# Interleaving four neighbouring tokens per partition in the attention stage of a fused attention, mixture-of-experts and feed-forward kernel

## Chip, cores and metric

The kernel runs on one core of one Trainium2 chip. The metric is the device time of one execution in microseconds (us). Three executions of the kernel before took 1749.69, 1757.17 and 1756.43 us, so the median is 1756.43.

## What is computed

```python
def _attn_ref(q, k, v):                       # (8, 8, 576, 64): batch, heads, tokens, head width
    k_p = k.reshape(B, H, 72, 8, D).mean(axis=3)
    v_p = v.reshape(B, H, 72, 8, D).mean(axis=3)
    scores = scale * np.matmul(q, k_p.transpose(0, 1, 3, 2))
    attn = softmax(scores)
    return np.matmul(attn, v_p)

x = attn_out.transpose(0, 2, 1, 3).reshape(B * S, H * D)      # 4608 tokens x 512
logits = x @ w_gate + np.log1p(np.exp(x @ w_noise)) * noise   # 8 experts, the best two are taken
out = sum over both: weight * (np.maximum(x @ w1[e], 0) @ w2[e])
h = out @ w_in;  g = h - np.tanh(h);  result = g @ w_out
```

Every token's row goes through attention, routing, its two experts and the last block by itself. The order in which tokens are put into tiles is therefore free, as long as the row of each token is read and written at its own place.

## The kernel before

The 4608 tokens are cut into 36 tiles of 128 tokens, one token per partition. A batch has 576 tokens, so a batch is 4.5 tiles long and two batches are nine tiles; tile 4 of each nine holds the end of one batch and the beginning of the next.

The program has three stages. `attention` (from line 1128) walks over the tiles and leaves each tile's 128 x 512 result in a DRAM buffer `x_d`, at row 128 t + partition. Beside it the router picks two experts per token and builds lists of row numbers. `moe` (from line 187) gathers rows of `x_d` by these lists, does the two layers of each expert and stores to `y_d`. `Moe2` (from line 659) gathers the two rows of each token, combines them and does the last block; line 1070 stores 128 result rows at a time to `out`.

The order of the work in `attention` is written out by hand in one loop over t (line 1713). One step t holds, among others: a load of q for tile t+4 (`load_q`, line 1184), the exponentials of tile t on ScalarE (`st_exps`, line 1362), the transposes of the attention weights of tile t-2 (`st_attT`, line 1387), the transposes of q of tile t+2 (`st_q`, line 1340), the scores of tile t+1 (`st_scores`, line 1348), jobs on k and v of a coming batch (line 1606 on), and the products with v of tile t-3 (`st_av`, line 1399). `st_g` (line 1421) scales the result of tile t-4 and stores it to `x_d`.

`load_q` issues one DMA on the queue of SyncE (SP) for each tile (two for a tile with two batches): 128 partitions x 8 heads x 64 elements, that is 1024 runs of 256 bytes. There are four buffers `qt`. The first four tiles are loaded ahead of the loop (lines 1207, 1208, 1237, 1240) between the loads of k and v of batches 0 and 1 (`load_kv`, line 1148). The noise of the router, 4608 x 8 numbers, is loaded at step 2 by one DMA (line 1662) in runs of 32 bytes.

In `st_q` the 512 columns of a q tile are transposed by four TensorE transposes of 128 x 128 (two heads each) into one PSUM tile `pt`, which ScalarE copies to `qT`:

```python
for m in range(HP):
    nc.tensor.transpose(p[:, m], qt[:, 2 * m:2 * m + 2].rearrange("s h d -> s (h d)"), identf)
QT[t] = wk.tile([128, HP, 128], F32, name="qT")
nc.scalar.activation(QT[t], p, AF.Copy)
```

A neighbour of it in form is `kbd` (line 1325), which multiplies a 64-column slice of the pooled k by a masked identity `parity`, so that the two products of a pair fill the lower and the upper 64 partitions of one PSUM tile (line 1331). The scores of a tile with two batches have the same form: 64-column slices of `qT`, lower and upper half in turn (line 1354).

SP's queue runs in program order and also carries the loads of k, v, weights and noise and the stores of `x_d`; each of its DMAs waits until the one eight before it has landed (the DMAHW entries in the order below).

Of the kernel before, what the change touches and what calls it, by code (L numbers as in the profile page):

```python
# [10 lines left out]
F32 = mybir.dt.float32  # L11
# [25 lines left out]
@with_exitstack  # L37
def kernel(ctx, tc, q, k, v, w_gate, w_noise, noise, w1, w2, w_in, w_out, out):
    nc = tc.nc
    B, H, S, D = q.shape  # L40
    N, E = noise.shape
    DM = H * D
    FF = w1.shape[2]
    F2 = w_in.shape[1]
    SP = S // 8
    NT = N // 128
    HP = H // 2
    ctx.enter_context(tc.manual_schedule())

    dram = ctx.enter_context(tc.tile_pool(name="dram", bufs=1, space=DRAM))  # L50
    x_d = dram.tile([N, DM], F32, name="x_d")
    y_d = dram.tile([(E + 1) * CAP + 128, DM], F32, name="y_d")
    ws_d = dram.tile([128, 2, 4, F2], F16, name="ws_d")
    const = ctx.enter_context(tc.tile_pool(name="const", bufs=1))

    identf = const.tile([128, 128], F32, name="identf")
    make_identity(nc, identf)
    onec = const.tile([128, 1], F32, name="onec")
    nc.vector.memset(onec, 1.0)
    ones1 = onec[0:1, 0:1].to_broadcast([1, 128])  # L60
    iota8 = const.tile([128, E], F32, name="iota8")
    nc.gpsimd.iota(iota8, pattern=[[1, E]], base=0, channel_multiplier=0, allow_small_or_imprecise_dtypes=True)
    tokid = const.tile([128, NT], I32, name="tokid")
    nc.gpsimd.iota(tokid, pattern=[[128, NT]], base=0, channel_multiplier=1)
    ridx = const.tile([128, NT, 2], I32, name="ridx")
    coef = const.tile([128, NT, 2], F32, name="coef")
    exps = const.tile([128, NT, 2, 1], F32, name="exps")
    poss = const.tile([128, NT, 2, 1], I32, name="poss")
    counts = const.tile([128, E], F32, name="counts")
    cnti = const.tile([1, 2 * E + 2], I32, name="cnti")  # L70
    idx = const.tile([128, E, NT], I32, name="idx")
    cin = const.tile([128, 4], F32, name="cin")
    wn2 = const.tile([1, 4], F32, name="wn2")
    outc = const.tile([128, DM], F32, name="outc")

    iscm = const.tile([128, 1], F32, name="iscm")
    hold = ctx.enter_context(tc.tile_pool(name="hold", bufs=1, side="right"))
    ew = ExitStack()
    early = ExitStack()
    pairs = [ew.enter_context(tc.tile_pool(name="ew0", bufs=1, side="right"))]  # L80
    ep = early.enter_context(tc.tile_pool(name="early", bufs=1, side="right"))
    x0T = ep.tile([128, 2, DM // 128, 512], F16, name="x0T")
    gate_ps = []
    W = {}
    V = dict(locals())
    with ExitStack() as st:
        attention(nc, tc, st, V)
    big = ctx.enter_context(tc.tile_pool(name="big", bufs=1))
    V["wi"] = big.tile([128, 2, 4, F2], F16, name="wi")
    V["wo"] = big.tile([128, 2, F2 // 128, DM], F16, name="wo")  # L90
    V["ps"] = ctx.enter_context(tc.tile_pool(name="m_ps", bufs=1, space=PSUM))
    z = Moe2(nc, tc, V)
    with ExitStack() as st:
        moe(nc, tc, st, V, z)
    ew.close()
    z.run(ctx)


def pow2(nc, m, x):
# [559 lines left out]
class Moe2:  # L659
# [165 lines left out]
    def main(self, near):  # L825
# [225 lines left out]
        def L2(j, f, blocks=range(4)):  # L1051
            g = G[j, f] if blocks[-1] < 3 else G.pop((j, f))
            for i in blocks:
                if f == 0:
                    PO[j, i] = ps.tile([128, DM], F32, name="py", bufs=4)
                p = PO[j, i]
                s = slice(128 * i, 128 * i + 128)
                nc.tensor.matmul(p, g[:, 0, s], wo[:, 0, f], start=(f == 0), stop=False)  # L1058
                nc.tensor.matmul(p, g[:, 0, s], wo[:, 1, f], start=False, stop=False)  # L1059
                nc.tensor.matmul(p, g[:, 1, s], wo[:, 0, f], start=False, stop=(f == KF - 1))  # L1060
            if f == KF - 1:
                for i in blocks:
                    o = wk.tile([128, DM], F32, name="o", bufs=5)
                    if i % 2:
                        nc.scalar.activation(o, PO.pop((j, i)), AF.Copy, scale=INV[j][:, i:i + 1])
                        tt(o, o, outc, op=OP.mult)
                    else:
                        stt(o, PO.pop((j, i)), INV[j][:, i:i + 1], outc, op0=OP.mult, op1=OP.mult)
                    r = 128 * (4 * j + i)
                    nc.sync.dma_start(self.out[r:r + 128, :], o)  # L1070

        if near:
            INV[0], ROW[0, 0] = self.first
# [8 lines left out]
        for u in range(len(units) + LAG):  # L1082
# [12 lines left out]
            if u < len(units):  # L1095
                j, f = units[u]
# [31 lines left out]
def attention(nc, tc, st, V):  # L1128
# [19 lines left out]
    def load_kv(b, nm, cs=((0, 3), (3, 5)), engs=(nc.sync,)):  # L1148
        a = KV[b, nm] = KVT[nm][b % 2]
        rows = dict(k=k, v=v)[nm][b].rearrange("h (s r) d -> (h s) r d", r=8)  # L1150
        for i, (c0, c1) in enumerate(cs):
            w = cuts[c1] - cuts[c1 - 1]
            engs[i % len(engs)].dma_start(a[:w, c0:c1], rows[cuts[c0]:cuts[c1]].rearrange("(c p) r d -> p c r d", p=w))
# [16 lines left out]
        a = KV[b, nm]  # L1170
        e.tensor_add(a[:, c, 0:n], a[:, c, 0:n], a[:, c, n:2 * n])

    QL = {}

    def runs(t):
        r, done = [], 0
# [4 lines left out]
            done += n  # L1181
        return r

    def load_q(t):
        qt = ld.tile([128, H, D], F32, name="qt", bufs=4)
        for o, n, b, s in runs(t):
            nc.sync.dma_start(qt[o:o + n], q[b, :, s:s + n, :].rearrange("h s d -> s h d"))
        QL[t] = qt

# [14 lines left out]
        for i in range(2):  # L1204
            nc.gpsimd.memset(KVT[nm][i][96:128, 3:5], 0.0)
    load_kv(0, "k", each, (nc.sync, nc.scalar))
    load_q(0)
    load_q(1)
    rowi = one.tile([128, 128], F32, name="rowi")
    nc.gpsimd.iota(rowi, pattern=[[1, 128]], base=0, channel_multiplier=-1, allow_small_or_imprecise_dtypes=True)  # L1210
    KB = [one.tile([128, 2 * HP * SP], F32, name=f"kb{i}") for i in range(2)]
# [22 lines left out]
    nc.gpsimd.iota(slot, pattern=[[1, 128]], base=0, channel_multiplier=0, allow_small_or_imprecise_dtypes=True)  # L1234
    lane = ep.tile([128, 1], F32, name="lane")
    nc.gpsimd.iota(lane, pattern=[[0, 1]], base=0, channel_multiplier=1, allow_small_or_imprecise_dtypes=True)
    load_q(2)
    load_kv(1, "k")
    load_kv(0, "v", each)
    load_q(3)  # L1240
    for w, o in ((w_gate, 0), (w_noise, E)):
        nc.sync.dma_start(wg[:, 0:H, o:o + E], w.rearrange("(h p) e -> p h e", p=64))
    load_kv(1, "v")
    nz = ep.tile([128, NT, E], F32, name="nz")
    for c in each:
# [94 lines left out]
    def st_q(t):  # L1340
        p = ps.tile([128, HP, 128], F32, name="pt", bufs=3)
        qt = QL.pop(t)
        for m in range(HP):
            nc.tensor.transpose(p[:, m], qt[:, 2 * m:2 * m + 2].rearrange("s h d -> s (h d)"), identf)
        QT[t] = wk.tile([128, HP, 128], F32, name="qT")
        nc.scalar.activation(QT[t], p, AF.Copy)

# [248 lines left out]
    def at(t, f, *a):  # L1596
        assert t >= 0
        at_step.setdefault(t, []).append((f, a))
# [38 lines left out]
    for b in range(1, B):  # L1637
# [21 lines left out]
        at_pe(T0, job["vt"])  # L1659
        at_pe(T0 + 1, job["vs"])  # L1660
        fixed(T0 + 1, 1800)
    at(2, lambda: nc.sync.dma_start(nz, noise.rearrange("(t p) e -> p t e", p=128)))

    def early_x():

# [46 lines left out]
    ex = []  # L1712
    for t in range(NT + 4):
        now[0] = t
        if t + 4 < NT:
            load_q(t + 4)
        if t < NT:
            st_exps(t)
        if t < 4:
# [89 lines left out]
```

## Time and profile before

| | |
|---|---|
| runs, us | 1749.69, 1757.17, 1756.43 (median 1756.43) |
| profiled execution | 1757.43 us, span 1755.6 us from the first to the last instruction |
| granted TensorE clock | 0.996 of full speed over the span |
| TensorE (PE) busy | 1723.1 us, 98% of the span |
| VectorE (DVE), ScalarE (ACT), GpSimd (POOL) busy | 1266.2, 922.9, 274.7 us |
| q loads | 40 DMAs on SP, 32 of 256 KB and 8 of 128 KB |
| last product of attention (line 1413) | starts at 208.89 us |
| first matmul of the experts (line 356) | starts at 211.72 us |

The profiled execution is 1.83 us longer than its span. An engine's busy time counts matmuls with modelled ends, so a PE that is busy need not be at its peak; how long a group of matmuls holds the PE is read from the start of its first to the start of the next group. Idle time of an engine is shown in square brackets with what ended it.

### The profile page before, as it was taken

What the parts mean: (1) busy time and instruction counts of PE and PEld (TensorE: products, weight loads), DVE (VectorE), ACT (ScalarE), POOL (GpSimd) and SP (SyncE); (2) the same over time, 40 slices, a digit from 0 to 9 for tenths busy, and PEclk for the clock granted to TensorE, in tenths of its full rate; (3) what the DMA queues carried; (4) which work ended last, traced back from release to release, by engine and by line L of the source; (5) the groups of instructions that cost most, each with busy time, mean ns of one, the idle gap of its engine ahead of it and who ended that gap; (6) DMA issues with size and microseconds to landing.
All of it is one profiled execution on the core that took longest, in us unless ns stands there. A gap on an engine that the chain in (4) does not pass through costs nothing.

```text
span 1755.6 us, 28446 instructions
## 1 busy us (share of the span) xinstructions
PE 1723.1 (98%) x10574; PEld 1040.4 (59%) x10576; DVE 1266.2 (72%) x2547; ACT 922.9 (53%) x2229; POOL 274.7 (16%) x267
## 2 busy tenths in 40 slices
PE   7999999999999999999999999999999999999997
PEld 5989855454454545445454544666666666666664
DVE  5789788766666676666564558688787978888775
ACT  5788634435243443434343446656575756657553
POOL 2443113131030301101010211102010101200000
PEclk9999999999999999999999999999999999999999
DMA  9998335645746464535643445223131304232100
GB/s 222 271 192 214 103 106 165 165 132 150 184 124 181 137 175 132 126 120 131 170 131 88 124 125 127 68 53 85 43 87 35 97 19 97 66 50 64 22 25 26
DMA packets 271413, 203.35 MB, mean 116 GB/s; under 512 B 188512, under 2 KB 222816, under 8 KB 271264
## 3 DMA queue, kind: packets, MB, share of 16 engines
q1 hardware_dynamic: 251808, 155.09, 33.9%
q0 software_dynamic: 19200, 45.89, 11.4%
q8 instruction: 85, 1.39, 0.3%
q14 instruction: 64, 0.52, 0.1%
q10 hardware_dynamic: 256, 0.46, 0.1%
HBM read 121.82 MB, written 45.74 MB: 95 GB/s over the span
## 4 chain that ended last, share of the span: by engine, by line
PE 91%; DMA 3%; DVE 3%; ACT 2%; SPq 1%; issue 1%; ACTq 0%; DVEq 0%
PE pt L917 10%; PE ph L356 7%; PE ph L917 7%; PE ph L358 7%; PE ph L357 7%; PE py L1058 7%; PE py L1059 7%; PE py L1060 7%; PE py L378 7%; PE py L379 7%; PE py L380 7%; PE px L1413 3%; PE py L385 1%; PE psc L1354 1%; DMA qt<-in_q 1%; DMA xTp<-xp 1%
## 5 line engine op out<-in xcount | busy, mean ns | idle before, releaser
L360 ACT ACTIVATE hT<-ph 128x512 f16<-128x512 f32 (+2 forms) x192 | 96.4, 504 | 400.3 <-PE ph L358 390.6
L356 PE MATMUL ph<-xTp,pair 128*128 128x384 f16 (+2 forms) x736 | 245.4, 333 | 2.9 <-DMA xTp<-xp 2.9
L357 PE MATMUL ph<-xTp,pair 128*128 128x384 f16 (+2 forms) x736 | 244.9, 333 | 0.0
L358 PE MATMUL ph<-xTp,pair 128*128 128x384 f16 (+2 forms) x736 | 244.9, 333 | 0.0
L361 DVE SCALAR_TENSOR_TENSOR hT<-ph,hT 128x512 f16<-128x512 f32 (+2 forms) x192 | 110.6, 576 | 182.8 <-ACT hT L360 181.1
L1060 PE MATMUL py<-wo,gT 128*128 128x512 f16 x576 | 218.3, 379 | 1.2 <-DVE gT L1007 1.2
L1058 PE MATMUL py<-wo,gT 128*128 128x512 f16 x576 | 218.3, 379 | 0.0
L378 PE MATMUL py<-pair,hT 128*128 128x512 f16 x576 | 218.3, 379 | 0.0
L380 PE MATMUL py<-pair,hT 128*128 128x512 f16 x576 | 218.3, 379 | 0.0
L379 PE MATMUL py<-pair,hT 128*128 128x512 f16 x576 | 218.3, 379 | 0.0
L1059 PE MATMUL py<-wo,gT 128*128 128x512 f16 x576 | 218.3, 379 | 0.0
L917 PEld LDWEIGHTS <-wi 128*128 128x128 f16 x1536 | 150.2, 98 | 58.5 <-DMA y<-yp 0.3
L315 POOL DMA_INDIRECT xg<-x_d,idx x75 | 79.1, 1055 | 653.1 <-DVE xp L342 480.8
L730 POOL DMA_INDIRECT y<-y_d,ridx x64 | 79.2, 1238 | 518.6 <-DVE y L741 278.2
L356 PEld LDWEIGHTS <-pair 128*128 128x128 f16 x768 | 75.0, 98 | 75.7 <-issue 12.9
L358 PEld LDWEIGHTS <-pair 128*128 128x128 f16 x768 | 75.1, 98 | 56.5
L357 PEld LDWEIGHTS <-pair 128*128 128x128 f16 x768 | 75.1, 98 | 56.0 <-issue 0.2
L1017 ACT ACTIVATE th<-th,bias 128x512 f32<-128x512 f32 x144 | 102.5, 712 | 3.4 <-DVE th L1015 3.2
L1018 DVE SCALAR_TENSOR_TENSOR th<-th,t 128x512 f32<-128x512 f32 x144 | 98.3, 683 | 1.4 <-ACT th L1017 1.4
L1014 DVE SCALAR_TENSOR_TENSOR t<-hb,cinf,hs 128x512 f32<-128x512 f32 x64 | 47.9, 749 | 71.0 <-ACT hs L1013 71.0
L1007 DVE TENSOR_TENSOR gT<-th,gT 128x512 f16<-128x512 f32 x144 | 98.4, 683 | 0.2 <-ACT gT L1006 0.2
L1060 PEld LDWEIGHTS <-gT 128*128 128x128 f16 x576 | 56.3, 98 | 69.5 <-DVE gT L1007 1.7
(319 smaller groups left out, 3415.6 us busy)
## 6 DMA issues: line engine op xcount, KB each, us to landing
stage<-in_moe_w SPq DMA_DIRECT2D x64, 512.0 KB
y_d<-ys SPq DMA_DIRECT2D x82, 256.0 KB
x_d<-xr SPq DMA_DIRECT2D x36, 256.0 KB
out<-o SPq DMA_DIRECT2D x36, 256.0 KB
qt<-in_q SPq DMA_DIRECT2D x32, 256.0 KB
raw<-in_moe_w_in SPq DMA_DIRECT2D x32, 256.0 KB
raw<-in_moe_w_out SPq DMA_DIRECT2D x32, 256.0 KB
ws_d<-ys SPq DMA_DIRECT2D x16, 256.0 KB
```

What stands on the lines that cost most here:

```text
L356: nc.tensor.matmul(p[:, :nt], w[:, 0, m, s], x[:, 0, m, :nt], start=(m == 0), stop=False)
L357: nc.tensor.matmul(p[:, :nt], w[:, 0, m, s], x[:, 1, m, :nt], start=False, stop=False)
L358: nc.tensor.matmul(p[:, :nt], w[:, 1, m, s], x[:, 0, m, :nt], start=False, stop=(m == KD - 1))
L361: stt(h[:, 1, :nt], p[:, :nt], 0.0, h[:, 0, :nt], op0=OP.max, op1=OP.subtract)
L378: nc.tensor.matmul(p, h[:, 0, s], w[:, 0, f], start=(f == 0), stop=False)
L379: nc.tensor.matmul(p, h[:, 0, s], w[:, 1, f], start=False, stop=False)
L380: nc.tensor.matmul(p, h[:, 1, s], w[:, 0, f], start=False, stop=(f == KF - 1))
L917: nc.tensor.matmul(p, w[:, a, m], y[:, c, b, m], start=(start and m + x == 0), stop=(m == 1 and x == 2), skip_group_check=True)
L1017: nc.scalar.activation(q, q, AF.Square, bias=bias[:, 2:3], scale=SP5)
L1058: nc.tensor.matmul(p, g[:, 0, s], wo[:, 0, f], start=(f == 0), stop=False)
L1059: nc.tensor.matmul(p, g[:, 0, s], wo[:, 1, f], start=False, stop=False)
L1060: nc.tensor.matmul(p, g[:, 1, s], wo[:, 0, f], start=False, stop=(f == KF - 1))
```

## The change

Four neighbouring tokens now share a partition. Of each nine tiles, tiles 0 to 3 hold 512 tokens of the first batch: partition p holds tokens 4p to 4p+3, and tile i takes the i-th of them. Tile 4 is as before (64 tokens of each batch, one per partition). Tiles 5 to 8 hold 512 tokens of the second batch like tiles 0 to 3. So q of four tiles is loaded together, in runs of 4 x 64 elements (1 KB); the noise of four tiles comes in runs of 128 bytes; a result tile's 128 rows are stored four rows apart. In the four-tile buffer two heads of one token are no longer neighbours, so each head is transposed alone, by a plain matmul with the identity, into the lower or upper half of `pt`.

```diff
+def token_rows(a, t):
+    g, u = divmod(t, 9)
+    r = 1152 * g + (512 if u == 4 else 640 * (u > 4))
+    if u == 4:
+        return a[r:r + 128, :]
+    return a[r:r + 512, :].rearrange("(p i) d -> p i d", i=4)[:, u % 5, :]
...
-                    r = 128 * (4 * j + i)
-                    nc.sync.dma_start(self.out[r:r + 128, :], o)
+                    nc.sync.dma_start(token_rows(self.out, 4 * j + i), o)
...
-    def load_q(t):
-        qt = ld.tile([128, H, D], F32, name="qt", bufs=4)
+    def load_q4(t, h=slice(0, H), i=slice(0, 4)):
+        b, s = divmod(t * 128, S)
+        if t not in QG:
+            QG[t] = ld.tile([128, H, 4, D], F32, name="qt4", bufs=2)
+            for j in range(4):
+                QL[t + j] = QG[t][:, :, j]
+        nc.sync.dma_start(QG[t][:, h, i], q[b, h, s:s + 512, :].rearrange("h (p i) d -> p h i d", i=4)[:, :, i])
+
+    def load_q1(t):
+        qt = ld.tile([128, H, D], F32, name="qt", bufs=1)
         for o, n, b, s in runs(t):
...
-    load_q(0)
-    load_q(1)
+    load_q4(0, i=slice(0, 2))
...
-    load_q(2)
+    load_q4(0, i=slice(2, 4))
+    load_kv(0, "v", each)
     load_kv(1, "k")
-    load_kv(0, "v", each)
-    load_q(3)
     for w, o in ((w_gate, 0), (w_noise, E)):
         nc.sync.dma_start(wg[:, 0:H, o:o + E], w.rearrange("(h p) e -> p h e", p=64))
+    load_q1(4)
+    load_q4(5)
     load_kv(1, "v")
...
         for m in range(HP):
-            nc.tensor.transpose(p[:, m], qt[:, 2 * m:2 * m + 2].rearrange("s h d -> s (h d)"), identf)
+            if t % 9 == 4:
+                nc.tensor.transpose(p[:, m], qt[:, 2 * m:2 * m + 2].rearrange("s h d -> s (h d)"), identf)
+                continue
+            for i in range(2):
+                nc.tensor.matmul(p[64 * i:64 * i + 64, m], qt[:, 2 * m + i], identf, start=True, stop=True, skip_group_check=True)
...
-    at(2, lambda: nc.sync.dma_start(nz, noise.rearrange("(t p) e -> p t e", p=128)))
+    def load_nz():
+        n, o = noise.rearrange("(g s) e -> s g e", s=2 * S), nz.rearrange("p (g t) e -> p g t e", t=9)
+        for t, s in ((0, 0), (5, S + 64)):
+            for g in range(B // 2):
+                nc.sync.dma_start(o[:, g, t:t + 4], n[s:s + 512, g].rearrange("(p i) e -> p i e", i=4))
+        nc.sync.dma_start(o[:, :, 4], n[512:640])
+
+    at(2, load_nz)
...
-        if t + 4 < NT:
-            load_q(t + 4)
+        for u, h in ((t + 6, slice(0, 4)), (t + 5, slice(4, 8))):
+            if 5 < u < NT and u % 9 in (0, 5):
+                load_q4(u, h)
+        if 4 < t + 4 < NT and (t + 4) % 9 == 4:
+            load_q1(t + 4)
```

On TensorE, at step 7 of the loop (transposes of the attention weights of tile 5, of q of tile 9, scores of tile 8, k of batch 2, products with v of tile 4), the order was:

```order
L1395 MATMUL pt<-identf,at 128x128 x3
L1395 MATMUL pt<-identf,at 96x128 x2
L1344 MATMUL pt<-identf,qt 128x128 x4
L1354 MATMUL psc<-kb_154,qT 128x144 x4
L1331 MATMUL pt<-parity,kt_109 64x128 x6
L1331 MATMUL pt<-parity,kt_109 64x96 x4
L1413 MATMUL px<-vb_155,aT 64x160
```

and is now (`qt_459` is the four-tile buffer of tiles 9 to 12):

```order
L1415 MATMUL pt<-identf,at 128x128 x3
L1415 MATMUL pt<-identf,at 96x128 x2
L1364 MATMUL pt<-identf,qt_459 64x128 x8
L1374 MATMUL psc<-kb_152,qT 128x144 x4
L1347 MATMUL pt<-parity,kt_109 64x128 x6
L1347 MATMUL pt<-parity,kt_109 64x96 x4
L1433 MATMUL px<-vb_153,aT 64x160
```

The third row went from four of 128 x 128 to eight of 64 x 128, the form of the ten matmuls of `kbd` two rows below it; it is so in 32 of the 36 tiles. Nothing else on TensorE, VectorE, ScalarE or GpSimd changed its place.

On SP's queue the start of the program was (kt_110 and vt_112 are k and v of batch 1, vt_111 is v of batch 0):

```order
L1187 DMA qt<-in_q 128x8x64 x3
L1153 DMA kt_110<-in_k 128x3x512
L1153 DMA kt_110<-in_k 96x2x512
L1153 DMA vt_111<-in_v 128x512 x3
L1153 DMA vt_111<-in_v 96x512 x2
L1187 DMA qt<-in_q 128x8x64
L1242 DMA wg<-in_moe_w_gate 64x8x8
L1242 DMA wg<-in_moe_w_noise 64x8x8
L1153 DMA vt_112<-in_v 128x3x512
L1153 DMA vt_112<-in_v 96x2x512
L1187 DMA qt<-in_q 64x8x64 x2
L1187 DMA qt<-in_q 128x8x64
```

and is now:

```order
L1198 DMA qt_147<-in_q 128x8x128 x2
L1161 DMA vt_111<-in_v 128x512 x3
L1161 DMA vt_111<-in_v 96x512 x2
L1161 DMA kt_110<-in_k 128x3x512
L1161 DMA kt_110<-in_k 96x2x512
L1256 DMA wg<-in_moe_w_gate 64x8x8
L1256 DMA wg<-in_moe_w_noise 64x8x8
L1203 DMA qt<-in_q 64x8x64 x2
L1198 DMA qt_190<-in_q 128x8x256
L1161 DMA vt_112<-in_v 128x3x512
L1161 DMA vt_112<-in_v 96x2x512
```

Four q tiles are loaded at once and ahead of all of batch 1 and of v of batch 0; v of batch 0 went ahead of k of batch 1; v of batch 1 now has five q tiles (4 to 8) in front of it.

On SP's queue at step 2, with the waits, the noise is now nine DMAs where one stood:

```order
L1171 DMA vt_111<-in_v 96x2x256 [waits DMAHW0_49,DVE_49]
L1687 DMA nz<-in_moe_noise 128x32 [waits DMAHW1_49]
L1687 DMA nz<-in_moe_noise 128x32 [waits DMAHW2_49]
L1687 DMA nz<-in_moe_noise 128x32 [waits DMAHW3_49]
L1687 DMA nz<-in_moe_noise 128x32 [waits DMAHW4_49]
L1687 DMA nz<-in_moe_noise 128x32 [waits DMAHW5_49]
L1687 DMA nz<-in_moe_noise 128x32 [waits DMAHW6_49]
L1687 DMA nz<-in_moe_noise 128x32 [waits DMAHW7_49]
L1687 DMA nz<-in_moe_noise 128x32 [waits DMAHW0_49]
L1688 DMA nz<-in_moe_noise 128x4x8 [waits DMAHW1_49]
L1198 DMA qt_459<-in_q 128x4x256 [waits DMAHW2_49,PE_49]
```

Each takes one of the eight places, so the q load behind them (tiles 9 to 12) is issued only after everything ahead of the noise has landed.

## Rows read from the trace of the kernel before

**Rows 1.** The page: its head, and the chain that ended last, by engine.

```profile
span 1755.6 us, 28446 instructions
...
PE 91%; DMA 3%; DVE 3%; ACT 2%; SPq 1%; issue 1%; ACTq 0%; DVEq 0%
```

**Rows 2.** Stretches: busy us (instructions) of PE, PEld, DVE, ACT, POOL; granted clock, DMA share, GB/s.

```profile
20.00:30.00 10.00, 7.42 (x42) 5.87 (x42) 5.57 (x10) 5.76 (x28) 0.00 (x0) 0.83 1.11 254
...
60.00:85.00 25.00, 23.76 (x202) 22.78 (x203) 19.03 (x41) 20.38 (x102) 10.13 (x11) 1.00 1.13 261
85.00:110.00 25.00, 24.48 (x212) 23.00 (x211) 20.87 (x68) 19.73 (x99) 11.45 (x12) 1.00 1.06 239
110.00:135.00 25.00, 22.60 (x186) 20.75 (x185) 19.28 (x50) 22.21 (x92) 8.91 (x11) 0.93 0.84 175
...
9.00:211.00 202.00, 185.67 (x1554) 171.40 (x1555) 160.36 (x431) 156.56 (x739) 66.01 (x70) 0.98 0.89 205
```

**Rows 3.** Timeline of PE: start, us, line, count, [idle before]; a step without jobs.

```profile
64.40 0.71 PE L1395 MATMUL pt<-identf,at 128*128 128x128 f32 x5
64.95 0.60 PE L1344 MATMUL pt<-identf,qt 128*128 128x128 f32 x4
65.39 1.15 PE L1354 MATMUL psc<-kb,qT 128*128 128x144 f32 x8
66.37 0.27 PE L1287 MATMUL pt<-identf,vm 128*1 128x128 f32 x1
```

**Rows 4.** Timeline of PE: groups of 64-column matmuls and what follows them.

```profile
55.24 1.21 PE L1331 MATMUL pt<-parity,kt 128*64 128x128 f32 x20 [0.32 <-ACT qT L1346]
56.25 2.94 PE L1413 MATMUL px<-vb,aT 128*64 128x160 f32 x24
...
76.23 1.21 PE L1331 MATMUL pt<-parity,kt 128*64 128x128 f32 x20
77.37 1.98 PE L1413 MATMUL px<-vb,aT 128*128 128x160 f32 x12
...
79.74 0.60 PE L1344 MATMUL pt<-identf,qt 128*128 128x128 f32 x4
80.27 1.20 PE L1354 MATMUL psc<-kb,qT 128*64 128x144 f32 x16
81.40 1.98 PE L1413 MATMUL px<-vb,aT 128*128 128x160 f32 x12
```

**Rows 5.** What PE waited for from 29 to 211 us: us, times, longest.

```profile
PE pt L1300 <- ACT aT L1396: 1.7, 2, 1.3
PE pt L1344 <- ACT aT L1396: 1.4, 1, 1.4
PE pt L1344 <- DMA qt<-in_q: 1.4, 1, 1.4
PE pt L1539 <- DVE l_row L1534: 1.2, 1, 1.2
PE pt L1495 <- DVE mb L1491: 0.7, 1, 0.7
PE pt L1287 <- ACT aT L1396: 0.7, 1, 0.7
PE pt L1331 <- POOL vb L1323: 0.6, 1, 0.6
```

**Rows 6.** What PE waited for from 0 to 29 us.

```profile
PE pt L1344 <- DMA qt<-in_q: 4.6, 2, 2.4
PE pt L1331 <- DVE kt L1171: 2.6, 1, 2.6
```

**Rows 7.** Timeline of DVE: the additions on v of batch 0 and of batch 1.

```profile
17.98 3.20 DVE L1171 TENSOR_TENSOR vt<-vt 128x256 f32<-128x256 f32 x7
...
33.10 1.48 DVE L1171 TENSOR_TENSOR vt<-vt 128x1280 f32<-128x1280 f32 x1
```

**Rows 8.** Timeline of PE: products with v after a wait.

```profile
119.69 3.52 PE L1413 MATMUL px<-vb,aT 128*128 128x160 f32 x12
```

More of the change, by code (lines that the diff above doesn't have):

```diff
@@ L1171, in add @@
         e.tensor_add(a[:, c, 0:n], a[:, c, 0:n], a[:, c, n:2 * n])
-    QL = {}
+    QL, QG = {}, {}
     def runs(t):
```

## Prediction, made before the run

> **What bounds the kernel now.** I read the page first: the chain that ended last is 91% TensorE (PE), and DMA has 3% of it [rows 1]. The change touches the attention stage (to about 211 us) and the address of the result rows, so I read that stage next, by stretches. Between 60 and 110 us the DMA engines are full (share 1.13 and 1.06), yet PE is busy 23.76 and 24.48 of 25 us [rows 2]. So in the steady state PE sets the pace and full DMA engines are hidden beneath it. Over 9 to 211 us PE is idle 202 - 185.67 = 16.3 us [rows 2]. The lists of waits say where: before 29 us 4.6 us in two waits for q and 2.6 for additions on k [rows 6]; after 29 us 9.1 us in eleven waits, of which one, 1.4 us, is for q [rows 5].
>
> **The change part by part.**
>
> *Loads of q.* They lose three quarters of their runs. What that can return is PE's waits for q: 4.6 + 1.4 us [rows 5, 6], not the DMA time. The wait of 1.4 after 29 us goes: -1.4. Of the two before, the loads in front of q of tiles 0 to 3 shrink from k(0), three q tiles, k(1) and v(0), 4.3 MB, to k(0), 1.2 MB. Tile 4 had k(0), k(1), v(0), v(1) and four q tiles in front, 5.8 MB, and now lacks v(1), 4.6 MB: at 254 GB/s [rows 2] some 5 us earlier. So the second wait (2.4) goes whole. Behind the first (2.2) stands another: VectorE adds on v(0) from 17.98 to 21.2 us [rows 7] and takes a maximum that PE needs next. I count 0.5 of it (between 0 and 2.2).
>
> *v(1) goes behind five q tiles.* 7.1 MB then have to land before it is whole, 28 us at that rate; it is used at 33.10 [rows 7]. Nothing, with 3 to 5 us in hand; VectorE, with the maxima of the scores queued behind the addition, and then PE would wait if it were late.
>
> *Transposes of q.* Four transposes hold PE from 64.95 to 65.39, 0.44 us [rows 3]. In 32 tiles eight matmuls with 64 columns replace them. That form is in the trace: the ten of `kbd` are shown as twenty, so eight become sixteen. Twenty (twelve of 128 columns, eight of 96: 2304 in all) take 56.25 - 55.24 = 1.01 us ahead of another 64-column group and 77.37 - 76.23 = 1.14 ahead of a full-width one [rows 4], so leaving the form costs 0.13. Entering it costs 0.09: the four transposes ahead of a 64-column group hold 80.27 - 79.74 = 0.53 instead of 0.44 [rows 3, 4]. Sixteen of 128 columns: 1.01 x 2048 / 2304 = 0.90, with both ends 1.12, or 0.68 more than now. From the two-batch scores: sixteen of 144 columns take 81.40 - 80.27 = 1.13 with the exit [rows 4], scaled to 128 columns 1.00, with the entry 1.09, or 0.65 more. I take **0.66 us per tile**. Lower end 0.46 (no ends), upper end 0.78 (1.13 unscaled, plus the entry).
> Of the 32 tiles, tile 0 lies ahead of the 2.6 us wait for k [rows 6] and is hidden, tile 3 lies in the wait that shrinks, and tiles 1 and 2 come before the scores that VectorE's chain starts from: +1.3. The other 28 stand in the full PE stream: 28 x 0.66 = **+18.5**.
> A rule of the Trainium skill prices this lower: TensorEngine Tiling (Array Packing), section When to Use Tiling, has a stationary operand of up to 64 columns run two at a time. By it sixteen take half of sixteen full-width ones, 16 x (0.98 / 8) x (128 / 144) / 2 = 0.87 us from the 0.98 of eight [rows 3]; 28 tiles would then cost 12.0 and the time would be 6.5 us below mine. I stay with the rows, where entry and exit are paid.
>
> *What the longer PE work swallows.* A wait for another engine shrinks if that engine's work is not itself started by the longer piece. Waits for ScalarE [rows 5]: at L1300 two (1.3 and 0.4), each shortened by up to 0.66: -1.1; at L1287 -0.6; the 1.4 at L1344 stays, since the copy it waits for hangs on scores that come after the transposes. Waits for VectorE and GpSimd, 1.2 + 0.7 + 0.6, gather lag over several steps: -2.0 of 2.5. After the wait of 1.3 near 117 us the granted clock of the stretch is 0.93 [rows 2] and twelve products take 3.52 us [rows 8] instead of 1.98 [rows 4]: part of them ran at the lower level, 1.2 GHz. I take back half of these 1.5: -0.8. Sum -4.5; all or nothing are the ends.
>
> *Noise.* Nine DMAs for one, each holding one of eight places, so the q load of tiles 9 to 12 waits for all ahead of it. These tiles are wanted five steps later, some 20 us. Nothing; without that cover a few us of waiting at tile 9.
>
> *Result rows four apart.* Still 128 runs of 2 KB per store; the only one on the path is the last. No row shows a strided store; I take nothing, 0.5 us either way. The experts gather rows by index before and after: nothing.
>
> *Sum.* Start: -0.5 - 2.4 + 1.3 = -1.6. Steady: +18.5 - 1.4 - 4.5 = +12.6. Together **+11.0 us**, all ahead of the experts' first matmul, which starts when attention's PE work ends. The profiled execution took 1757.43 (span 1755.6 [rows 1]), 1.0 above the median of 1756.43, so 1768.4 there and 1767 against the median. Lower end: 28 x 0.46 = 12.9, less all 9.1 + 1.5 and the 4.6 at the start: -2.3, 1754. Upper end: 28 x 0.78 = 21.8, less 1.4: +20.4, 1777.
>
> **The rivals.** A measurement of this kernel tells 0.5%, 8.8 us, from no change: below 1747.6 is faster, above 1765.2 slower.
>
> *The gaps swallow most of it.* Lower end of the price and every wait but the 1.4 at L1344 and 1.1 of small ones shortened: 12.9 at the steady tiles, start -0.5 - 2.4 + 0.9, swallowed 1.4 + 1.3 + 2.5 + 1.5: +4.2, 1761. For it: after 135 us VectorE has much to do too, so lag is likely; against it: both measured 64-column groups pay their ends. Chance 0.41.
>
> *Slow loads set the pace (the other side).* If PE's waits all come from loads that run late under full DMA engines, by way of k, v and stores, 1 KB runs return the 16.3 us and, with the slow clock of rows 8 (1.5) and of 20 to 30 us (0.83 [rows 2], some 0.9), 18.7 in all. Faster then follows once a tile's transposes add less than (18.7 - 8.8) / 28 = 0.35 us; at 0.23, half my lower end, 18.7 - 6.4 = 12.3 less, 1744. For it: DMA shares above 1. Against it: of the waits after 29 us only 1.4 us name a load, and no row prices the 64-column form that low. DMA: Bandwidth & Descriptors, section Specifications, puts line rate at transfers of 512 bytes and more, which by itself speaks for this rival; the PE share beside full DMA engines is what speaks against it. Chance 0.05.
>
> *SP's queue runs dry at the noise.* While nine small DMAs fill the places, no large one is in flight; if then halves of k and v of batch 2 come late, PE waits at tile 9. Price: like the waits for q seen so far, two of 2.4 [rows 6]: +11.0 + 4.8, 1772. Against it: the margin of 20 us. Chance 0.10.
>
> **How the numbers follow.** My forecast, 1767, has 0.44. Slower by over 0.5%: 0.44 + 0.10 = 0.54; within: 0.41; faster: 0.05. That two signs are close is because +11.0 lies just past 8.8. The range takes in the swallowed case and the dry queue and nearly both ends: 1756 to 1776.
>
> **What would show it.** Right: from the first of sixteen q matmuls to the next group 1.05 to 1.15 us; no wait of PE for q; experts start near 222 us; later stages of equal length. Wrong: a q group below 0.9 us; PE waits for v(1) or for tile 9; PE idle after 29 us above 9 us although q is there; a last store that lands later than before.

## The result, and the profile after

| | before | after |
|---|---|---|
| median of 8 runs each (us) | 1757.05 | 1766.59 |
| lowest to highest (us) | 1749.69 to 1761.98 | 1763.23 to 1771.32 |
| profiled execution, span (us) | 1757.43, 1755.6 | 1771.32, 1769.5 |
| experts' first matmul (us) | 211.72 | 223.11 |
| from there to the end of the span (us) | 1543.9 | 1546.4 |

The ratio after to before is 1.0064, 95% interval [1.0044, 1.0083]: slower by 0.64%. The profiled execution of after is the longest of its eight, 4.7 us over their median, so single steps of its trace are told beside a second execution below.

The page of after, head, DMA packets and chain, answers to [rows 1]:

```profile
span 1769.5 us, 29159 instructions
...
DMA packets 244647, 203.39 MB, mean 115 GB/s; under 512 B 152528, under 2 KB 196048, under 8 KB 244496
...
PE 94%; DVE 2%; DMA 1%; ACT 0%; issue 0%; POOL 0%; SPq 0%; another core or an unknown queue 0%; POOLq 0%; DVEq 0%; ACTq 0%
```

DMA has gone from 3% of the chain (the work that ended last) to 1%, and PE from 91% to 94%. The DMA packets were 271413 before. The change does what it says to the loads, and PE pays for it. Two of the stretches of [rows 2], from the windows view (columns as there):

```profile
60.00:85.00 25.00, 25.00 (x238) 22.74 (x237) 17.72 (x38) 18.97 (x94) 8.58 (x10) 1.00 0.84 222
...
9.00:211.00 202.00, 194.90 (x1846) 173.14 (x1847) 151.45 (x404) 152.72 (x728) 65.82 (x69) 0.99 0.79 198
```

The DMA share between 60 and 85 us fell from 1.13 to 0.84, and PE's idle time over 9 to 211 us from 16.3 to 7.1 us. Both would read as a gain to whoever looks at busy shares alone; but PE is fuller because a tile costs it more. Nor does the share between 60 and 85 us fall because of the longer runs: it is 0.82 in run 1 below, with the old loads, and 1.15 in run 2, with the new ones and the old transposes. The timeline of PE in after, two steps without jobs (answers to [rows 3]):

```profile
96.86 0.71 PE L1415 MATMUL pt<-identf,at 128*128 128x128 f32 x5
97.50 1.09 PE L1364 MATMUL pt<-identf,qt 128*64 128x128 f32 x16
...
101.44 0.71 PE L1415 MATMUL pt<-identf,at 128*128 128x128 f32 x5
```

and the same step of the kernel before:

```profile
93.40 0.71 PE L1395 MATMUL pt<-identf,at 128*128 128x128 f32 x5
93.95 0.60 PE L1344 MATMUL pt<-identf,qt 128*128 128x128 f32 x4
...
97.20 0.71 PE L1395 MATMUL pt<-identf,at 128*128 128x128 f32 x5
```

From one `at` group to the next the step takes 101.44 - 96.86 = 4.58 us, and took 97.20 - 93.40 = 3.80: **0.78 us more**. The `at` group ahead holds PE for 0.64 instead of 0.55, so 0.09 is entry. The q group itself is seen here:

```profile
65.35 1.09 PE L1364 MATMUL pt<-identf,qt 128*64 128x128 f32 x16
66.37 1.25 PE L1374 MATMUL psc<-kb,qT 128*128 128x144 f32 x8
67.45 0.27 PE L1303 MATMUL pt<-identf,vm 128*1 128x128 f32 x1
```

It holds PE 66.37 - 65.35 = 1.02 us instead of 0.44 [rows 3], 0.58 more; the full-width scores behind it hold 1.08 instead of 66.37 - 65.39 = 0.98, so 0.10 of the exit lies there. 0.09 + 0.58 + 0.10 = 0.77.

Where the scores behind q are themselves 64 columns wide (the next tile is shared by two batches), there is no exit to pay:

```profile
81.06 0.71 PE L1415 MATMUL pt<-identf,at 128*128 128x128 f32 x5
81.70 1.09 PE L1364 MATMUL pt<-identf,qt 128*64 128x128 f32 x16
82.62 1.15 PE L1374 MATMUL psc<-kb,qT 128*64 128x144 f32 x16
83.70 1.98 PE L1433 MATMUL px<-vb,aT 128*128 128x160 f32 x12
```

Here q holds PE 0.92 us instead of 0.53, and the scores 1.08 instead of 1.13 [rows 4]. With the 0.09 of entry the step takes 0.43 more (0.44 from one `at` group to the next); four of the 28 steps are of this kind.

What PE waited for in after, before 29 us (answers to [rows 6]):

```profile
PE pt L1347 <- DVE kt L1179: 2.0, 1, 2.0
PE pt L1303 <- DVE vm L1299: 1.5, 1, 1.5
...
```

and from 29 to 225 us (answers to [rows 5]):

```profile
PE pt L1559 <- DVE l_row L1554: 0.8, 1, 0.8
PE pt L1306 <- DVE vx L1309: 0.8, 1, 0.8
PE pt L1515 <- DVE vx L1309: 0.8, 1, 0.8
PE pt L1316 <- ACT aT L1416: 0.5, 1, 0.5
...
```

No wait of either list names q any more. The first of the old waits for q (2.2) is in part replaced by one for VectorE's maximum of v (1.5), as the prediction had it. The profiled spans differ by 1769.5 - 1755.6 = 13.9 us: 11.4 arise ahead of the experts' first matmul and 2.5 behind it, where PE stands 5.6 us at the experts' `xTp` (the list of waits names no releaser for it), and stood 2.9 in the kernel before, for a load. The other executions below need 1541 to 1545 us for that part, so these 2.5 belong to this one execution.

### The profile page after: what moved, and what is told of

Same layout as the page of the kernel before. It is cut to its first block, busy times and chain, and to the rows that moved or that the text cites. A ratio compares the mean times of both kernels' runs of the same rounds, so it can differ in the third digit from the quotient of the medians.

```text
span 1769.5 us, 29159 instructions
## 1 busy us (share of the span) xinstructions
PE 1746.0 (99%) x10960; PEld 1052.8 (59%) x10960; DVE 1266.5 (72%) x2547; ACT 924.4 (52%) x2229; POOL 275.5 (16%) x267
## 4 chain that ended last, share of the span: by engine, by line
PE 94%; DVE 2%; DMA 1%; ACT 0%; issue 0%; POOL 0%; SPq 0%; another core or an unknown queue 0%; POOLq 0%; DVEq 0%; ACTq 0%
PE pt L926 9%; PE ph L365 7%; PE ph L367 7%; PE ph L366 7%; PE ph L926 7%; PE py L1067 7%; PE py L1069 7%; PE py L1068 7%; PE py L387 7%; PE py L388 7%; PE py L389 7%; PE px L1433 4%; PE psc L1374 2%; PE pt L1364 2%; PE py L394 1%; PE pt L1415 1%
```

## Experiments

Each ratio is against runs of the kernel before on the same chip. "To the experts" is the start of the experts' first matmul in the profiled execution, 211.72 before.

**1. The 64-column form alone.** The kernel before, with only this edit:

```
-            nc.tensor.transpose(p[:, m], qt[:, 2 * m:2 * m + 2].rearrange("s h d -> s (h d)"), identf)
+            if t % 9 == 4:
+                nc.tensor.transpose(p[:, m], qt[:, 2 * m:2 * m + 2].rearrange("s h d -> s (h d)"), identf)
+                continue
+            for i in range(2):
+                nc.tensor.matmul(p[64 * i:64 * i + 64, m], qt[:, 2 * m + i], identf, start=True, stop=True, skip_group_check=True)
```

> The kernel before, with its own loads and token order, whose 32 q tiles outside the two-batch ones are transposed by eight 64-column matmuls in place of four full-width transposes. Nothing else of the change is in it. My theory (the longer transposes stand in the full PE stream): 28 tiles x 0.675 us = 18.9 (0.675 is 1.025 + 0.09 - 0.44 from the changed kernel's trace), 1.3 for tiles 1 and 2, less some 5 to 6 that shortened waits swallow, the wait of 1.4 for q among them: +14 to +15, near 1771.5, experts' first matmul near 226 us instead of 211.7. Rival 1 (the gaps swallow most): +4 to +6. Rival 2 (loads set the pace, so PE work hides under them): 0 to +3.

Measured: 1767.72 us (6 runs), ratio 1.0086 [1.0073, 1.0098]. Its timeline at the experts:

```profile
226.70 0.38 PE L356 MATMUL ph<-x0T,pair 128*128 128x512 f16 x1 [0.38 <-DVE lg L1442]
```

To the experts 226.70, 15.0 later than before, as the theory had it; both rivals' numbers are missed. The matmuls by themselves make the kernel as slow as the whole change does, within the intervals. The steps without jobs are 0.78 us longer here too, and those ahead of two-batch scores 0.44. 24 x 0.78 + 4 x 0.44 = 20.5, and tiles 1 and 2 add 1.3 ahead of them; so 6.8 are taken back without any help from the new loads.

The edit changes two things at once: the operation (a plain matmul for a transpose) and its width (64 columns for 128). The Trainium skill's Perfetto Trace Analysis, section Transposes, asks for the transpose operation and not a standard matmul. This run goes the way of that sentence, with 15 us in this kernel, but it does not separate the two. Each alone can be estimated from the trace of the kernel before, which has transposes of 64 columns in `vt`:

```profile
66.48 0.71 PE L1290 MATMUL pt<-identf,vt 128*64 128x128 f32 x5
67.02 1.88 PE L1413 MATMUL px<-vb,aT 128*128 128x160 f32 x12
```

Five of them hold PE 0.54 us, 0.11 each, like full-width ones (0.44 / 4 [rows 3]); eight would take about 0.87. Four plain matmuls of full width, by the 0.98 of four scores [rows 3], would take 0.98 x 128 / 144 = 0.87 as well. So by these estimates either change alone nearly doubles the 0.44, and the two together make it 1.02. No run tried one without the other.

**2. The loads alone.** The change, with four full-width transposes on two tokens of one head, so that q's columns are paired otherwise than the scores want them:

```
-            for i in range(2):
-                nc.tensor.matmul(p[64 * i:64 * i + 64, m], qt[:, 2 * m + i], identf, start=True, stop=True, skip_group_check=True)
+            j = (t % 9) % 5
+            w = QG[t - j][:, 2 * m + j % 2, 2 * (j // 2):2 * (j // 2) + 2].rearrange("p i d -> p (i d)")
+            nc.tensor.transpose(p[:, m], w, identf)
```

> The changed kernel with all its loads, noise and stores, but with four full-width transposes per q tile again. They take 128 neighbouring columns of the four-tile buffer, which are two tokens of one head and not two heads of one token, so q rows are mixed up and the result is not the reference's; the amount of work is that of the kernel before. My theory: only the waits for q return, some 2.9 at the start and 1.4 later: -4 (-2 to -6), near 1753, experts' first matmul near 207. Rival 2 (loads set the pace): all waits of PE return, -16, near 1741, first matmul near 196. Rival 3 (the queue runs dry at the noise): a wait of PE at tile 9 appears, and nothing is gained.

Measured: 1752.32 us (12 runs) against 1752.01, ratio 1.0004 [0.9994, 1.0014]; to the experts 211.67. The expected 4 us are not there. By step, the start of the `at` group less that of the kernel before is -4.4 us at step 9 (60.00 against 64.40 [rows 3]), -2.1 at step 12, -2.4 at step 19, -0.3 at step 22 and -0.1 at step 37. So the loads do give a lead, and most of it is lost in two places, both on PE's timeline of this run:

```profile
72.60 0.63 PE L1361 MATMUL pt<-identf,qt 128*128 128x128 f32 x4 [1.66 <-DMA qt<-in_q]
...
114.98 0.38 PE L1316 MATMUL pt<-vx,onec 1*128 1x1 f32 x2 [1.33 <-ACT aT L1417]
118.25 3.65 PE L1434 MATMUL px<-vb,aT 128*128 128x160 f32 x12
```

The first is q of tile 13, shared by two batches and loaded only four steps ahead, behind a whole group. The second is the wait for ScalarE that stood in the kernel before, and behind it the stretch at the lower clock, longer than before (3.65 us for the products instead of 3.52 [rows 8]). The windows view of this run there, and of after at the same products:

```profile
115.00:120.00 5.00, 5.00 (x28) 4.77 (x29) 2.17 (x11) 4.11 (x19) 3.63 (x7) 0.60 0.02 5
```

```profile
125.00:130.00 5.00, 5.00 (x49) 4.83 (x49) 3.80 (x13) 4.52 (x21) 5.00 (x9) 1.00 0.18 14
```

The granted clock is 0.60 after 1.33 us of waiting in the one (0.50, the lower level of 1.2 GHz, from 117 to 121 us), and 1.00, the upper level, after a wait of 0.5 in the other. The length of that wait does not decide it, though. PE's timeline has the wait and the products of that place in run 1, and in run 8 below:

```profile
125.03 0.38 PE L1300 MATMUL pt<-vx,onec 1*128 1x1 f32 x2 [0.55 <-ACT aT L1400]
...
127.28 3.25 PE L1417 MATMUL px<-vb,aT 128*128 128x160 f32 x12
```

```profile
118.08 0.38 PE L1316 MATMUL pt<-vx,onec 1*128 1x1 f32 x2 [1.34 <-ACT aT L1422]
...
120.33 1.92 PE L1439 MATMUL px<-vb,aT 128*128 128x160 f32 x12
```

Run 1 waits as short a time as after and its products run at the lower clock (0.59 from 127 to 131 us); run 8 waits as long as the kernel before, and its products take the 1.92 us that they take in after, at the upper clock (1.00 from 120 to 124 us). What decides it stays open.

The rival in which slow loads set the pace is ruled out: with those loads and the old transposes the time is unchanged, where it had 16 us less.

**3. One DMA for the noise**, in 32-byte runs as before the change (the values then belong to other tokens):

```
-    at(2, load_nz)
+    at(2, lambda: nc.sync.dma_start(nz, noise.rearrange("(t p) e -> p t e", p=128)))
```

> The changed kernel with the noise loaded by one DMA in runs of 32 bytes as before, so that the noise goes to other tokens of the same tiles. My theory: SP stood 10.4 us at the nine noise DMAs in the changed kernel's trace, but PE did not wait: 0 +- 1 us against the changed kernel, first expert matmul at 223 +- 1. Rival 3 (the nine DMAs starve the queue): 3 to 5 us less than the changed kernel. A rival the other way: one DMA of 4608 short runs holds the DMA engines longer, and PE waits for q or k near 40 us, +1 to +3.

Measured: 1765.81 us (4 runs), ratio 1.0072 [1.0057, 1.0087]; to the experts 223.02. The timeline of SP in after shows what the nine cost there:

```profile
23.83 9.74 SPq L1687 DMA_DIRECT2D nz<-in_moe_noise  x8
...
34.36 0.61 SPq L1198 DMA_DIRECT2D qt<-in_q  x1
```

and that of SP in this run, with one:

```profile
23.52 0.88 SPq L1690 DMA_DIRECT2D nz<-in_moe_noise  x1
24.49 9.14 SPq L1198 DMA_DIRECT2D qt<-in_q  x1
```

With one DMA the q load behind it stands for the same 9 us, so SP's stop there does not come from the number of noise DMAs. In after the list of SP's waits names landings of k and v for 5.7 of the 10.4 us, that is, places taken by the large loads ahead. In run 3 it names TensorE for the whole 9.2, although the last tile in the load's buffer had been transposed by 22.1 us; that the places are the cause there too is likely, not shown. The dry queue of the prediction did not occur.

**4. Result rows stored neighbouring** (they then stand at other tokens' places):

```
-                    nc.sync.dma_start(token_rows(self.out, 4 * j + i), o)
+                    nc.sync.dma_start(self.out[128 * (4 * j + i):128 * (4 * j + i) + 128, :], o)
```

> The changed kernel with each result tile stored to 128 neighbouring rows as before, so that the rows of the result stand in another order. My theory: the same time as the changed kernel within 1 us, and the time from the experts' first matmul to the end within 1 us of the kernel before (1543.9). Rival: the strided stores cost; then this kernel is 0.5 to 2.5 us faster than the changed one, whose time from the experts' first matmul to the end was 2.5 us longer than before.

Measured: 1765.11 us (4 runs), ratio 1.007 [1.0056, 1.0085]. From the experts' first matmul to the end 1543.5 us, against 1543.9 before: storing rows four apart costs nothing that can be seen.

**5. The change again**, on the chip of the next three.

> The changed kernel once more, beside the next three on one chip. Expected: 12 to 14 us over the kernel before, as with the two kernels that differ from it only in the noise loads and in the stores (1765.81 and 1765.11 against 1752.01).

Measured: 1766.53 us (4 runs), ratio 1.0072 [1.0051, 1.0094]; to the experts 221.25, 1.9 sooner than in the first profile. 1.6 of that difference arise between 30 and 36 us. The `at` group there, in the first profile of after

```profile
32.14 1.27 PE L1415 MATMUL pt<-identf,at 128*128 128x128 f32 x5
```

and in this one

```profile
31.54 0.71 PE L1415 MATMUL pt<-identf,at 128*128 128x128 f32 x5
```

The windows view of this stretch has a granted clock of 0.57 in the first profile and of 1.00 in this one:

```profile
30.50:34.50 4.00, 4.00 (x27) 2.65 (x25) 2.13 (x2) 3.69 (x20) 3.66 (x4) 0.57 0.56 84
```

```profile
30.50:34.50 4.00, 3.84 (x48) 3.07 (x46) 2.72 (x4) 4.00 (x21) 3.22 (x3) 1.00 0.73 139
```

**6. The halves apart.** The change, with the four lower halves of a tile first and then the four upper ones:

```
-        for m in range(HP):
...
             for i in range(2):
-                nc.tensor.matmul(p[64 * i:64 * i + 64, m], qt[:, 2 * m + i], identf, start=True, stop=True, skip_group_check=True)
+                for m in range(HP):
+                    nc.tensor.matmul(p[64 * i:64 * i + 64, m], qt[:, 2 * m + i], identf, start=True, stop=True, skip_group_check=True)
```

> The change with its eight 64-column matmuls of a tile in another order: the four that fill the lower 64 rows of the PSUM tile first, then the four that fill the upper. Theory: 1.02 us for the group of eight is so little because neighbouring ones, which go to different halves, run side by side; a pair then takes 0.256 us. With the halves apart, each would take that by itself, the group some 2.0 us, and 28 tiles 27 us more: the experts' first matmul near 250 us. Rival: a 64-column matmul takes 0.128 us whatever stands beside it: no difference (within 2 us).

Measured: 1778.70 us (one run). PE's timeline:

```profile
62.68 1.58 PE L1365 MATMUL pt<-identf,qt 128*64 128x128 f32 x16
64.19 1.25 PE L1375 MATMUL psc<-kb,qT 128*128 128x144 f32 x8
...
235.04 0.38 PE L365 MATMUL ph<-x0T,pair 128*128 128x512 f16 x1 [0.38 <-DVE lg L1459]
```

Neither theory's number. The group holds PE 64.19 - 62.68 = 1.51 us, not 2.0 and not 1.02. The order within the tile is worth 0.49 us; 28 x 0.49 = 13.7, and to the experts it is 235.04 - 221.25 = 13.8 more than in run 5. That also shows that further time added to the q group comes through to the experts in full, once the waits are used up.

**7. GpSimd regroups.** From tile 3 on GpSimd copies a tile's columns side by side, three steps ahead, and PE transposes the copy in four full-width pieces:

```
+    def side_by_side(t):
+        if 2 < t < NT and t % 9 != 4:
+            w = ld.tile([128, H, D], F32, name="qw", bufs=2)
+            nc.gpsimd.tensor_copy(w, QL[t])
+            QL[t] = w
...
-            if t % 9 == 4:
+            if t % 9 == 4 or t > 2:
...
+        side_by_side(t + 3)
         if t < NT:
             st_exps(t)
```

> The change, but from tile 3 on GpSimd copies the tile's four-apart columns into a tile of its own, three steps ahead, and TensorE makes four full-width transposes from that as before the change; tiles 0 to 2 keep the 64-column form. Theory that the price of the 64-column form is all that the change costs, and that its loads by themselves give nothing: experts' first matmul within 1.5 us of 211.7 us, time within 3 us of the kernel before. Rival: GpSimd stands up to 24 us in all at its additions for k, waiting for loads, and the copies queue behind these; TensorE then waits for them, 2 to 6 us in all, and the time lies that much over the kernel before.

Measured: 1758.17 us (12 runs) against 1752.57, ratio 1.003 [1.0019, 1.0042]; to the experts 218.83. Of the change's 14 us it takes back 8.4. What is left is in PE's waits of this run, which are the rival's by size, but most of them not by place:

```profile
PE pt L1521 <- DVE mb L1517: 2.9, 2, 1.5
PE pt L1316 <- ACT aT L1422: 2.8, 3, 1.5
PE pt L1367 <- POOL qw L1359: 1.6, 1, 1.6
...
```

One wait, 1.6 us, is for a copy; the longer ones are for VectorE and ScalarE. Some of VectorE's own operations got longer beside the copies, here the group that grew most, in the kernel with copies and in that of run 2 (29 to 211 us, one form alone; busy us, mean ns, idle before):

```profile
L1500 DVE SCALAR_TENSOR_TENSOR g_p<-g_p,g_th 128x80 f32<-128x80 f32 x18 | 8.4, 466 | 0.3
```

```profile
L1495 DVE SCALAR_TENSOR_TENSOR g_p<-g_p,g_th 128x80 f32<-128x80 f32 x18 | 5.5, 305 | 0.3
```

Most groups kept their time, the largest among them (maxima of the scores, 451 ns here and 452 in run 2).

**8. The same, and q of the two-batch tile six steps ahead:**

```
-        qt = ld.tile([128, H, D], F32, name="qt", bufs=1)
+        qt = ld.tile([128, H, D], F32, name="qt", bufs=2)
...
-        if 4 < t + 4 < NT and (t + 4) % 9 == 4:
-            load_q1(t + 4)
+        if 4 < t + 6 < NT and (t + 6) % 9 == 4:
+            load_q1(t + 6)
```

> The kernel with GpSimd's copies, and the q tile that two batches share is loaded six steps ahead instead of four, into one of two buffers. Theory that the loads' lead of 4.4 us at step 9 was lost in part at that tile, to a wait of 1.7 us at tile 13: that wait goes, and the experts' first matmul comes 1 to 2 us sooner than in the kernel with copies alone. Rival: the lead is lost wherever TensorE comes to the next wait, at ScalarE's copies of the weights near step 19 with the clock falling after it: no difference (within 0.5 us).

Measured: 1758.30 us (11 runs), ratio 1.0032 [1.0022, 1.0041]. The medians of 7 and 8 differ by 0.1 us, which is the rival's number. But in run 7's profile PE did not wait for that tile's q, so this pair could not test the point it was made for. The single profile, 214.48 to the experts and so 4.4 sooner than run 7, does not show in the medians; 1.7 of it is the clock at the products behind the wait near 118 us (1.92 us here, 3.65 in run 7).

**9. Interleaved tiles, q in 256-byte runs.** The change, but a tile's heads lie side by side in SBUF, so four full-width transposes serve:

```
-            QG[t] = ld.tile([128, H, 4, D], F32, name="qt4", bufs=2)
+            QG[t] = ld.tile([128, 4, H, D], F32, name="qt4", bufs=2)
...
-        nc.sync.dma_start(QG[t][:, h, i], q[b, h, s:s + 512, :].rearrange("h (p i) d -> p h i d", i=4)[:, :, i])
+        for j in range(4)[i]:
+            nc.sync.dma_start(QG[t][:, j, h], q[b, h, s:s + 512, :].rearrange("h (p i) d -> p h i d", i=4)[:, :, j])
...
```

> The change's interleaved tiles, noise and stores, and its loading in groups of four tiles, but each tile lies in SBUF with its heads side by side: q comes in 256-byte runs as before the change (one load per tile and half of the heads), and TensorE makes four full-width transposes from it. Theory that the price of the 64-column form is all that the change costs, and that the length of the runs sets nothing here: time within 2 us of the kernel before, experts' first matmul within 1.5 us of 211.7 us. Rival: the 1 KB runs are what keeps the waits for q away, and groups of four tiles in 256-byte runs land late: waits of TensorE for q of 2 us or more in all beyond those of the loads alone (1.7 us), and the time as much over the kernel before.

Measured: 1763.63 us (6 runs, 1758.2 to 1769.11) against 1753.09, ratio 1.0057 [1.0034, 1.0079]. The theory's number is missed; to the experts it is 214.41, 2.7 later than before. The profiled execution, 1758.71, is near the lowest of the six; in it PE waits, by the list of waits from 29 us on:

```profile
PE pt L1361 <- DMA qt<-in_q: 3.7, 1, 3.7
PE px L1430 <- DVE lg L1455: 2.6, 1, 2.6
...
```

and SP's timeline ahead of the first of them:

```profile
54.31 9.75 SPq L1199 DMA_DIRECT2D qt<-in_q  x4
...
71.25 2.95 SPq L1204 DMA_DIRECT2D qt<-in_q  x2
```

Tile 13's q, issued by 71.25 + 2.95 = 74.2 us, was wanted at 74. So run 2's loads, which set no pace, become late once a group of four tiles comes in short runs and four times as many DMAs. Which of the two does it was not tried, and the further 5 us between this profile and the median are not shown.

**10. The kernel before with more lead.** Nothing of the change; q 2, q 3 and v(0) ahead of k(1) at the start, q loaded five tiles ahead into six buffers:

```
     load_q(2)
+    load_q(3)
+    load_kv(0, "v", each)
     load_kv(1, "k")
-    load_kv(0, "v", each)
-    load_q(3)
...
-        if t + 4 < NT:
-            load_q(t + 4)
+        for u in (4, 5) if t == 0 else (t + 5,):
+            if u < NT:
+                load_q(u)
```

> The kernel before with the start's loads in another order (q of tiles 2 and 3 and batch 0's v ahead of batch 1's k) and q loaded five tiles ahead instead of four, into six buffers instead of four; nothing else of the change. Theory that TensorE's lead from loads is lost at the next wait, as it was with the change's loads alone: within 2 us of the kernel before. Rival: the waits for q at the start (2.9 us) and after 29 us (1.4 us) were a loss of their own: 3 to 4 us faster.

Measured: 1752.15 us (12 runs) against 1753.09, ratio 1.0 [0.9986, 1.0014]. Its profile, the shortest of the twelve, has no wait for q and reaches the experts at 207.17, 4.5 sooner; the medians differ by 0.9. The theory's time holds, but its mechanism is not in this profile: the `at` group of step 9 starts 3.9 us ahead of the kernel before, and that of the last step 4.6, so no later wait took the lead back. Why the median stays is not shown. No version found here is faster than the kernel before.

## Why the prediction was right

The forecast was 1767 and slower; the median is 1766.59, with +11.4 us to the experts where +11.0 was worked out. The mechanism held: the loads were hidden, the transposes were not. That the sum came so close is partly luck, since two of its terms were off in opposite ways, by 2.0 and 1.6 us, and since the executions differ: beside run 5 the same change is 14.0 us over the kernel before, and here 9.5, with intervals that overlap.

- *The price of 0.66 per tile* was too low: 0.78 in the 24 steps whose scores are full width (where no wait takes some of it back), 0.44 in the four ahead of two-batch scores, in after as in run 1. That makes 24 x 0.78 + 4 x 0.44 = 20.5 instead of 18.5. The term that was mis-sized is the exit. The scaling to 128 columns held: it gave 0.90 ahead of another 64-column group, and 0.92 is measured. But the exit was read inside the group alone, as 0.13, and the other part of it lies in the full-width group behind, which the prediction put at nothing. The trace of the kernel before has it:

```profile
62.69 1.88 PE L1413 MATMUL px<-vb,aT 128*128 128x160 f32 x12
...
79.19 0.71 PE L1395 MATMUL pt<-identf,at 128*128 128x128 f32 x5
```

  Products behind full-width scores hold PE 64.40 - 62.69 = 1.71 [rows 3], behind `kbd` 79.19 - 77.37 = 1.82 [rows 4], so 0.1 more. With it the prediction's first sum is 0.68 + 0.10 = 0.78, as measured. Its sign of being right, a q group of 1.05 to 1.15, was missed for the same reason: 1.02, or 0.92.
- *The rule that was weighed*, of the Trainium skill, TensorEngine Tiling (Array Packing), section When to Use Tiling, gave an estimate of 0.87 for that group. Measured are 0.92 and 1.02 in alternating order and 1.51 with the halves apart. So the bare group in alternating order comes near it; what its 12.0 us left out are the ends, 0.09 ahead of the group and up to 0.20 at its end.
- *What is taken back* was too small by about as much. By the steps of the trace 20.5 - 11.4 = 9.1 came back, and the prediction had 1.6 + 1.4 + 4.5 = 7.5. By place: up to step 4, 0.3 (run 5: 2.0) of 1.6; steps 5 and 8, 3.2; step 19, with the slow products, 2.3; the rest 3.3, in portions of up to 0.7, mostly where the kernel before waited for ScalarE or VectorE.
- *The gaps swallow most of it*, the rival at 0.41, had 2.0 at the start and 6.7 later, 8.7 in all, nearer to the 9.1 than the forecast was. It missed by its price, 0.46 per tile against 0.73 in the mean.
- *"The 1.4 at L1344 stays"* was wrong. That wait for ScalarE in step 5 [rows 5] is gone in after, in run 1 (longer PE work, old loads), in run 2 (new loads, old PE work) and in run 10: either a later PE or an earlier start removes it. It makes 1.6 of the 3.2 above. (The "eleven waits" of 9.1 us are eleven rows of the list, with thirteen waits in them.)
- *The clock* came back whole: in after the twelve products at that place take 1.92 us instead of 3.52 [rows 8], 1.6 where 0.8 was taken, and so they do in run 5. In run 1, after as short a wait, they still take 3.25. So no ground of the prediction tells which of the two it would be; that all of it came back is luck as far as these runs show.
- *Wait for q after 29 us, v(1) late, noise, strided stores*: as predicted; runs 3 and 4 show the last two at nothing.
- *The loads' return.* The prediction booked 0.5 + 2.4 + 1.4 for them. Run 2 shows that alone they return nothing (ratio 1.0004 [0.9994, 1.0014]), since other waits follow. Beside the slower PE, after is 3.6 us ahead of run 1 at the experts; by the medians, each over that of the kernel before on its chip, run 1 stands at +15.7 and after at +9.5 and (run 5) +14.0, with intervals that overlap, so how much of the 3.6 lasts stays open. *Slow loads set the pace* had 0.05 and is refuted. The sentence beside it named DMA: Bandwidth & Descriptors of the Trainium skill, section Specifications, which puts line rate at transfers of 512 bytes and more. With the longer runs of run 2 the DMA share over 9 to 211 us is 0.80 at 204 GB/s, instead of 0.89 at 205 [rows 2], which goes the way of that sentence; the time did not change.

## What to carry to other kernels

Before a layout is changed for the sake of longer DMA runs, look at what bounds the stage: a DMA share above 1 beside an engine that is 95% busy is hidden, and that engine pays the price of the new layout, less what its waits take back (here 9.1 of 20.5 us). Price a changed operand form by the step from one fixed group to the same group of the next step, not by the group alone: of 0.78 us, 0.19 lay in the neighbours. A lead that faster loads give is worth what no later wait takes back: run 2's was gone before the experts. And a lead in one profile is not yet a shorter median: run 10's profile kept its lead, and the median of its twelve runs is that of the kernel before.

## What the runs showed of the hardware that was not expected

- Eight fp32 matmuls with 64 stationary and 128 moving columns hold TensorE 1.02 us ahead of full-width work (0.92 ahead of another such group) when neighbours go to different halves of the PSUM partitions, and 1.51 us ahead of full-width work when four go to one half and then four to the other. The full-width groups on both sides are longer by 0.09 and 0.10 us.
- A transpose of 64 columns holds TensorE 0.11 us, as long as one of 128.
- The same place of the program ran at either clock: after a wait of 0.55 us at the upper one in after and at the lower one in run 1, after 1.34 us at the lower one in the kernel before and at the upper one in run 8.
- One group of VectorE's operations on 128x80 took 466 ns in the mean instead of 305 in the kernel whose GpSimd makes 29 copies of 128x512 more (85.5 us busy instead of 66.0 over 9 to 211 us); most other groups kept their time. That the copies are the cause is the near reading; it was not tried by itself.
- Profiled executions of one kernel reach the experts up to 2 us apart (223.11 and 221.25), with a granted clock of 0.57 and of 1.00 in the stretch from 30.5 to 34.5 us.
